# A gelu tail dealt out anew between ScalarE, VectorE and GpSimd, and two sums taken in turns, in the last block of an attention and MLP kernel

## The chip, the cores and the metric

The kernel runs on one core of one Trainium2 chip. The metric is the device time of one execution in microseconds (us). Of several executions the median counts. Beside them stands one profiled execution with its trace.

## The reference

The reference is one transformer layer with adaptive layer norms, for 2048 rows of 512 numbers, all in float32:

```
mod = (silu(c) @ w_mod) -> sa, ca, ga, sb, cb, gb
h = layernorm(x) * (1 + ca) + sa
x = x + ga * attention(h)         # 32 query heads of 16, one key and value head
h = layernorm(x) * (1 + cb) + sb
x = x + gb * (gelu(h @ w1 + b1) @ w2 + b2)     # gelu by tanh; w1 is 512 x 1376
```

What follows is about the last line: the MLP, and in it the gelu and the second product, `@ w2`.

## The kernel before

**Blocks.** The 2048 rows are worked in eight blocks of 256. For each block there is attention, and then a job that the kernel calls `rest`: output projection (`wops`), layer norm, first MLP product (`w1ps`), gelu, second MLP product (`w2ps`), store. While attention of block b runs, TensorE takes small batches of matmuls from the job of block b-1. For the last block, 7, there is no attention left to lie beside; its job runs alone at the end, and many lines in it ask `if fast`. This document is about that end.

**Numbers in two parts.** Each float32 operand of a projection or MLP product is split into a high part, a cast to the narrower `fp32r` type, and a low part, the remainder after that cast. The function `split` (line 128) issues the two instructions: a cast (lines 130 to 134, by engine) and a subtraction (line 137). A product of two such operands is three matmuls: high by high, low by high, high by low. `batches` (line 167) lists these matmuls in order and hands them out in lists of a given size; before a list goes out it asks `ready` whether the last chunk in it has been issued, and gives out a wait of one step (`yield -1`) as long as it has not.

**Chunks.** The 1376 columns of `w1` are 11 chunks of 128 (`NF` = 11, the last one padded). For one chunk, the first product is 12 matmuls with 256 columns (four parts of 512 rows, times three). The first four chunks (`GROUP`) go together, row part by row part, since the parts of the normed input come one after another; chunks 4 to 10 follow one by one. The gelu of one chunk is a 128 x 256 tile and, in the last block, this row of instructions:

| step after the chunk's turn | engine and line | what |
|---|---|---|
| 1 | ScalarE 947 | `z` = sum + bias, out of PSUM |
| 1 | ScalarE 948 | `tt` = its square, scaled, out of PSUM |
| 1 | VectorE 949 | `tt` = (`tt` + 1) * `z` |
| 4 | ScalarE 960 | `tt` = tanh of it, scaled |
| 6 | VectorE 964 | `z` = (`tt` + 1) * `z` |
| 6 | VectorE, by `split`, 134 | `gH` = cast of `z` |
| 6 | VectorE or GpSimd, by `split`, 137 | `gL` = `z` - `gH`: VectorE for even chunks and for 9 and 10, GpSimd for 1, 3, 5 and 7 |

**The second product.** Each of the two 128-row halves of the block is a sum over the 11 chunks, 33 matmuls, in which the gelu is the stationary operand and `w2` the moving one. The first half has 512 columns. The second half is made as two sums of 256 columns, so that the last store is short. The three sums come one after another: all of the first, all of the second, all of the third. Each is then added to the input rows by VectorE (line 1009) and sent out (line 1010).

**What sets the order.** The program is written with a manual schedule: every engine, and the queue of DMAs on SP, runs its instructions in the order in which the Python code issues them, and waits on semaphores for what each needs. That order follows a counter of steps, `clock`. `later(n, fn)` (line 145) appends `fn` to the list `pending` with the step `clock + n`; `due` (line 151) runs everything that has come due, in the order of that list. In the end phase (lines 1471 to 1484) the last job's generator is walked: a list of matmuls is issued at once and takes no step; a number n is n steps, and each step (`tick`) takes one batch of the job that is still open, that of block 6, issues it, counts one on, and runs `due`. Each chunk of the last block's first product ends with `later(1, gelu)` and two steps, so that in step 2f the second product, cast and remainder of chunk f-3 and the tanh of chunk f-2 are issued, and in step 2f+1 the bias, square and first product of chunk f.

**Fillers.** Two gaps at the start of the last block's job, where its operands are still on their way, are filled with what is left of block 6's second product: `TAIL` = (4, 3) gives four steps and then three, one batch each; one more batch of six (`left`, line 914) is put between the transposes (`PARTS`).

**PSUM banks.** The last block's sums take banks in a fixed turn (`spread`, line 728, and `bank`, line 731).

Of the kernel before, what the change touches and what calls it, by code (L numbers as in the profile page):

```python
# [8 lines left out]
F32 = mybir.dt.float32  # L9
F32R = mybir.dt.float32r  # L10
AF = mybir.ActivationFunctionType
ALU = mybir.AluOpType
AX = mybir.AxisListType

P = 128
# [18 lines left out]
BATCH = 6  # L34
SHORT = 4
LONG = (3, 1)
TAIL = (4, 3)
PARTS = (2, 4)
GROUP = 4
NORM_WAIT = 6  # L40
WARM = (4, 16, 2, 5)
# [4 lines left out]
def raw(ap):  # L46
    return ap.bitcast(F32)
# [3 lines left out]
def adaln_mqa_mlp(  # L51
# [15 lines left out]
    nc = tc.nc  # L67
    _, S, D = x.shape
# [10 lines left out]
    NF = (F + P - 1) // P  # L79
# [4 lines left out]
    blocks = [(r, HQ) for r in range(0, S, HQ)]  # L84
# [43 lines left out]
    def split(dst_h, dst_l, src, eng_h, eng_l, between=None):  # L128
        if eng_h is nc.gpsimd:
            eng_h.tensor_scalar(out=dst_h, in0=src, scalar1=1.0, scalar2=0.0, op0=ALU.mult, op1=ALU.add)  # L130
        elif eng_h is nc.scalar:
            eng_h.copy(dst_h, src)
        else:
            eng_h.tensor_copy(out=dst_h, in_=src)  # L134
        if between:
            between()
        eng_l.tensor_tensor(out=dst_l, in0=src, in1=raw(dst_h), op=ALU.subtract)  # L137
# [7 lines left out]
    def later(n, fn):  # L145
        if draining[0]:
            fn()
        else:
            pending.append((clock[0] + n, fn))
# [17 lines left out]
    def batches(ps, pairs, size, ready=lambda n: True, begin=True, end=True):  # L167

        todo = [(a, b_) for wh, wl, xh, xl in pairs for a, b_ in ((wh, xh), (wl, xh), (wh, xl))]
        last = len(todo) - 1  # L170

        ends = list(range(len(todo), 0, -size))[::-1]
        if ends[0] == 1:
            ends.pop(0)
        for begin_, end_ in zip([0] + ends, ends):
            part = range(begin_, end_)
            while not ready(part[-1] // 3):
                yield -1
            yield [(ps, *todo[n], begin and n == 0, end and n == last) for n in part]

    def whole(batch):
        for ps, a, b_, first_, last_ in batch:
            nc.tensor.matmul(ps, a, b_, start=first_, stop=last_)  # L183
# [622 lines left out]
    def rest_steps(b, fast, rp, bank, ons, ready):  # L806
# [4 lines left out]
        for hf in range(w // HQ):  # L811
# [53 lines left out]
                for h in range(2):  # L865
                    later(3 - 2 * t + 2 * h, lambda t=t, h=h: stats(t, h))
            if fast:
                yield TAIL[0]
                for t in range(2):
                    yield from batches(pss[t], out_pairs(t, [KD - 1]), BATCH, begin=False)  # L870
                    add_x(t, pss[t])
                    stats(t, 0)
                    stats(t, 1)
                    rstd(t, t + 1)
                for t in range(2):
                    xhat(t)
                yield TAIL[1]
            if not fast:
                later(4, lambda: rstd(0, 2))
                later(5, lambda: xhat(0))  # L880
# [31 lines left out]
            if fast:  # L912
                tps = [psum.tile([P, 2, HQ], F32, name=f"tp2_{b}_{hf}_{dp}", **bank()) for dp in range(KD // 2)]
                left = take()
                assert len(left) == sum(PARTS)
                for t in range(2):
                    for dp in range(KD // 2):
                        turn2(dp, tps[dp], t)
                    whole(left[:PARTS[t]])
                    left = left[PARTS[t]:]  # L920
                for dp in range(KD // 2):
                    modulate(dp, tps[dp])
                advance()
                for t in range(2):
                    add_bias(t)
                yield MOD_WAIT
            else:
                for dp in range(KD // 2):
                    ps = psum.tile([P, 2, HQ], F32, name=f"tp2_{b}_{hf}_{dp}", **bank())
                    yield [(ps[:, d2, t * P:(t + 1) * P], xh[:, t, (2 * dp + d2) * P:(2 * dp + d2 + 1) * P], ident,  # L930
                            t + d2 == 0, t + d2 == 2) for t in range(2) for d2 in range(2)]
                    modulate(dp, ps)
                whole_h = clock[0] + 4
                state.update(busy=False, turns=2)
# [7 lines left out]
            def gelu(f, ps):  # L942
                odd = fast and f % 2
                z = rp.tile([P, HQ], F32, name=f"z{b}_{hf}_{f}", tag="wf" if odd else "z", bufs=3)
                tt = rp.tile([P, HQ], F32, name=f"tt{b}_{hf}_{f}", tag="h322" if odd else "tt", bufs=2)
                if fast:
                    nc.scalar.activation(z, ps, AF.Identity, bias=b1c[:, f:f + 1])
                    nc.scalar.activation(tt, ps, AF.Square, scale=GELU_R, bias=b1r[:, f:f + 1])
                    nc.vector.scalar_tensor_tensor(out=tt, in0=tt, scalar=1.0, in1=z, op0=ALU.add, op1=ALU.mult)
                else:  # L950
                    nc.vector.tensor_scalar(out=z, in0=ps, scalar1=b1c[:, f:f + 1], scalar2=None, op0=ALU.add)
                    later(1, lambda: inner(z, tt))

                def inner(z, tt):
                    nc.scalar.activation(tt, z, AF.Square, scale=GELU_R)  # L955
                    nc.gpsimd.tensor_scalar(out=tt, in0=tt, scalar1=1.0, scalar2=1.0, op0=ALU.mult, op1=ALU.add)  # L956
                    nc.gpsimd.tensor_tensor(out=tt, in0=tt, in1=z, op=ALU.mult)  # L957

                def tanh():
                    nc.scalar.activation(tt, tt, AF.Tanh, scale=GELU_C)  # L960

                def last():
                    if fast:
                        nc.vector.scalar_tensor_tensor(out=z, in0=tt, scalar=1.0, in1=z, op0=ALU.add, op1=ALU.mult)
                    else:
                        nc.gpsimd.tensor_tensor(out=tt, in0=tt, in1=z, op=ALU.mult)  # L966
                        nc.gpsimd.tensor_tensor(out=z, in0=tt, in1=z, op=ALU.add)  # L967
                    split(gH[:, f, :], gL[:, f, :], z, nc.vector if fast else nc.gpsimd,
                          nc.vector if fast and (f % 2 == 0 or f > NF - 3) else nc.gpsimd)
                    made.add(f)  # L970

                later(3 if fast else 4, tanh)
                later(5 if fast else 6, last)
# [32 lines left out]
            def store(t, ps, cols=slice(0, D)):  # L1006
                row = row0 + hf * HQ + t * P
                ot = rp.tile([P, D], F32, name=f"ot{b}_{hf}_{t}", tag="ot", bufs=2)
                nc.vector.tensor_tensor(out=ot[:, cols], in0=ps[:, :cols.stop - cols.start], in1=x1[:, t, cols], op=ALU.add)
                send = lambda: nc.sync.dma_start(out=of[row:row + P, cols], in_=ot[:, cols])  # L1010
                if fast:
                    send()
                else:
                    later(2, send)

            while weights:
                yield 2
            for t in range(2):
                sl = slice(t * P, (t + 1) * P)
                for cols in (slice(0, D // 2), slice(D // 2, D)) if fast and t else (slice(0, D), ):  # L1020
                    place = dict(tag="m", bufs=3) if b == len(blocks) - 2 and t else bank()
                    ps = psum.tile([P, D], F32, name=f"w2ps{b}_{hf}_{t}_{cols.start}", **place)
                    ops = [(gH[:, f, sl], gL[:, f, sl], w2H[:, f, cols], w2L[:, f, cols]) for f in range(NF)]
                    size_ = SHORT if b == len(blocks) - 2 and not t else BATCH
                    yield from batches(ps[:, :cols.stop - cols.start], ops, size_, lambda f: made.issuperset(range(f + 1)))
                    if fast:
                        later(1, lambda t=t, ps=ps, cols=cols: store(t, ps, cols))
                        yield 2
                    else:
                        store(t, ps)  # L1030
        stage[b] = 2

    stage = {}
# [127 lines left out]
    def advance():  # L1161

        for job in holder or list(queue):
            while not held and job[0] <= clock[0] and go_on(job):
                pass
            if held or holder:
                break
# [4 lines left out]
    def take():  # L1172
        advance()
        return held.pop() if held else None
# [293 lines left out]
    end_step(*behind)  # L1468
    last = queue.pop()[1]

    def tick():

        batch = take()
        if batch:
            whole(batch)
            advance()
        clock[0] += 1
        due()

    for r in last:  # L1480
        if isinstance(r, list):
            whole(r)
        else:
            for _ in range(max(abs(r), 1)):
                tick()
# [33 lines left out]
```

## Time and profile before

| | us |
|---|---|
| median of three runs | 1560.76 |
| the three runs | 1559.91 to 1560.95 |
| the profiled execution, its own time | 1559.96 |
| span of its trace, first to last instruction | 1557.8 |

Busy over that span are TensorE 1541.8 us, VectorE 1401.4, ScalarE 1228.2 and GpSimd 687.2. TensorE's granted clock is 1.00 throughout. The span leaves out 2.2 us of the execution's own time.

In rows of a timeline, the first number is the start in us from the span's start, the second the length in us, then engine, line, operation, and the tiles as output<-inputs with their shapes; in brackets stands how long the engine was idle ahead of it and what ended that. PE is TensorE (PEld its loads of weights), DVE VectorE, ACT ScalarE, POOL GpSimd. A row of a chain has start, length, engine, tile, line and count. A row of waits has who waited for whom, the total in us, the count and the longest. Lengths of instructions that overlap can't be added; the distance between starts tells the pace.

### The profile page before, as it was taken

The numbers are of one execution on the slowest core, as the hardware profiler recorded it, in microseconds if no ns is written. First come the engines' busy times: TensorE is split into PE (matmuls) and PEld (weight loads), VectorE is DVE, ScalarE is ACT, GpSimd is POOL, SyncE is SP. The second block draws the span as 40 slices with busy tenths as digits, with TensorE's granted clock in tenths as the row PEclk, the third lists the DMA queues.
The fourth block names the chain that finished last, engine by engine and source line by source line (L and its number), as shares of the span: only waits on it lengthen the run. The fifth ranks groups of instructions, "written<-read, shape, count | busy, mean of one in ns | idle before, by whom it ended". The sixth has DMA issues, their size and how long they took to land.

```text
span 1557.8 us, 41408 instructions
## 1 busy us (share of the span) xinstructions
PE 1541.8 (99%) x16372; PEld 953.8 (61%) x16372; DVE 1401.4 (90%) x2476; ACT 1228.2 (79%) x2392; POOL 687.2 (44%) x1198
## 2 busy tenths in 40 slices
PE   7999999999999999999999999999999999999999
PEld 4455555567655665557655675556655576556658
DVE  7999999999999999999999999999999999999725
ACT  5577778788878887788877887788877888778963
POOL 5545433867322571246521562245612474225722
PEclk9999999999999999999999999999999999999999
DMA  7235412312030211203112120303112130212241
GB/s 241 101 94 199 146 56 86 124 52 97 19 109 20 83 58 37 94 21 106 31 51 80 55 87 23 108 15 100 44 47 83 35 108 16 74 63 64 83 144 70
DMA packets 83269, 121.61 MB, mean 78 GB/s; under 512 B 19630, under 2 KB 56494, under 8 KB 82820
## 3 DMA queue, kind: packets, MB, share of 16 engines
q1 hardware_dynamic: 83060, 118.97, 23.6%
q8 instruction: 129, 2.11, 0.6%
q14 instruction: 64, 0.52, 0.1%
q10 hardware_dynamic: 16, 0.00, 0.0%
HBM read 91.13 MB, written 27.27 MB: 76 GB/s over the span
## 4 chain that ended last, share of the span: by engine, by line
PE 88%; DVE 10%; DMA 2%; ACT 1%; issue 0%; POOL 0%; SPq 0%; DVEq 0%
PE acc L633 30%; PE m L507 25%; PE e L612 16%; DVE mx L512 8%; PE w1ps L193 8%; PE w2ps L183 2%; PE w2ps L193 2%; PE qps L193 2%; PE w1ps L183 1%; DMA xt<-in_A_x_dram 1%; PE tp L193 1%; PE wops L193 1%; PE kps L162 1%; DVE st L833 1%; DVE x L826 1%; PE idle L287 0%
## 5 line engine op out<-in xcount | busy, mean ns | idle before, releaser
L512 DVE TENSOR_REDUCE mx<-m 128x1 f32<-128x512 f32 x2048 | 1269.1, 681 | 87.0 <-PE m L507 65.7
L616 ACT ACTIVATE p<-e 128x512 f32<-128x512 f32 x2048 | 1098.4, 598 | 253.9 <-PE e L612 115.7
L507 PE MATMUL m<-ks,qst 64*128 64x512 f32 x2048 | 831.4, 429 | 1.6 <-DVE mx L512 0.6
L612 PE MATMUL e<-qst,ks 64*128 64x512 f32 x2048 | 739.9, 412 | 0.0
L633 PE MATMUL acc<-p,va 128*32 128x256 f32 x8192 | 548.0, 385 | 0.0
L507 PEld LDWEIGHTS m<-ks,qst 64*128 64x128 f32 x2048 | 366.2, 184 | 209.8 <-DVE mx L512 174.0
L612 PEld LDWEIGHTS e<-qst,ks 64*128 64x128 f32 x2048 | 358.0, 184 | 92.2 <-ACT p L616 63.6
L633 PEld LDWEIGHTS acc<-p,va 128*32 128x32 f32 x8192 | 213.8, 109 | 214.2 <-issue 110.7
L555 POOL TENSOR_SCALAR mt<-turned 8x32 f32<-8x32 f32 x256 | 53.5, 209 | 417.9 <-DVE turned L561 405.9
L193 PE MATMUL w1ps<-h2H,w1t 64*128 64x256 f32 x1216 | 232.9, 287 | 0.0
L193 PEld LDWEIGHTS w1ps<-h2H,w1t 64*128 64x128 f32 x1216 | 183.5, 185 | 28.5 <-DVE mx L512 16.9
L193 PE MATMUL w1ps<-h2L,w1t 64*128 64x256 f32 x608 | 167.2, 275 | 0.0
L193 PE MATMUL w2ps<-w2H,gH 64*128 64x512 f32 x264 | 115.9, 439 | 0.0
L193 PEld LDWEIGHTS w1ps<-h2L,w1t 64*128 64x128 f32 x608 | 112.3, 185 | 0.0
L193 PE MATMUL w2ps<-w2L,gH 64*128 64x512 f32 x264 | 103.5, 392 | 0.0
L193 PE MATMUL w2ps<-w2H,gL 64*128 64x512 f32 x264 | 102.9, 390 | 0.0
L956 POOL TENSOR_SCALAR tt<-tt 128x256 f32<-128x256 f32 x77 | 31.2, 405 | 141.1 <-ACT tt L955 107.9
L137 POOL TENSOR_TENSOR gL<-z,gH 128x256 fp32r<-128x256 f32 x81 | 60.6, 748 | 17.4 <-DVE gH L134 11.0
L957 POOL TENSOR_TENSOR tt<-tt,z 128x256 f32<-128x256 f32 x77 | 56.9, 739 | 6.4
L967 POOL TENSOR_TENSOR z<-tt,z 128x256 f32<-128x256 f32 x77 | 56.5, 734 | 6.0
L966 POOL TENSOR_TENSOR tt<-tt,z 128x256 f32<-128x256 f32 x77 | 56.7, 736 | 0.0
L193 PE MATMUL wops<-woH,onH 64*128 64x512 f32 x112 | 49.7, 443 | 0.0
(188 smaller groups left out, 1505.0 us busy)
## 6 DMA issues: line engine op xcount, KB each, us to landing
w1t<-dw SPq DMA_DIRECT2D x82, 512.0 KB
qst<-dq SPq DMA_DIRECT2D x384, 32.0 KB
do<-oc SPq DMA_DIRECT2D x64, 128.0 KB
dw<-w1s SPq DMA_DIRECT2D x11, 512.0 KB
xt<-in_A_x_dram SPq DMA_DIRECT2D x4, 1024.0 KB
dq<-qH SPq DMA_DIRECT2D x16, 256.0 KB
dq<-qL SPq DMA_DIRECT2D x16, 256.0 KB
x<-in_A_x_dram SPq DMA_DIRECT2D x8, 512.0 KB
```

The costliest lines, as they stand in the source:

```text
L137: eng_l.tensor_tensor(out=dst_l, in0=src, in1=raw(dst_h), op=ALU.subtract)
L183: nc.tensor.matmul(ps, a, b_, start=first_, stop=last_)
L193: ins = nc.tensor.matmul(ps, a[rows], b_[rows], start=first_ and s == 0, stop=last_ and s == 1)
L507: nc.tensor.matmul(m, qsts[u][rows, j, t * P:(t + 1) * P], ks[rows, kc * 512:(kc + 1) * 512], start=True, stop=True)
L512: nc.vector.tensor_reduce(out=self.mx[u][:, i, kc:kc + 1], in_=m, axis=AX.X, op=ALU.max)
L555: nc.gpsimd.tensor_scalar(out=mt[:, g:g + 32], in0=turned[g:g + 4 * T, :], scalar1=1.0, scalar2=0.0, op0=ALU.mult, op1=ALU.add)
L612: nc.tensor.matmul(e, ks[rows, kt * P:(kt + 1) * P], rhs, start=True, stop=True)
L616: ins = nc.scalar.activation(dst, e, AF.Exp, scale=0.25)
L633: ins = nc.tensor.matmul(accs[u][32 * cidx:32 * cidx + 32, :], va[:, kt, :], rhs, start=kt == 0, stop=kt == NKT - 1)
L957: nc.gpsimd.tensor_tensor(out=tt, in0=tt, in1=z, op=ALU.mult)
L966: nc.gpsimd.tensor_tensor(out=tt, in0=tt, in1=z, op=ALU.mult)
L967: nc.gpsimd.tensor_tensor(out=z, in0=tt, in1=z, op=ALU.add)
```

## The change

Four things change, all in the last block or in the end phase.

- The number of steps in the two gaps is unchanged, four and three, but the matmuls of block 6 are dealt out to them by number: 5, 4, 4, 4 and 6, 6, 6. A new function `some` takes them one by one out of the batches. A plain step no longer takes a batch.
- For chunks 0 to 8 the high part `gH` is made by ScalarE (`nc.scalar.copy`), issued in the place where the cast stood.
- For the same chunks the low part `gL` is made by VectorE, one step later, for odd and even chunks alike. Chunks 9 and 10 keep VectorE for both, as before.
- The three sums are issued in pieces: chunks 0 to 5 of the first sum, chunks 0 to 5 of the second, chunks 6 to 10 of the first, chunks 6 to 10 of the second, then the whole third sum.

```
-TAIL = (4, 3)
+TAIL = ((5, 4, 4, 4), (6, 6, 6))
+SOON = 6
...
-                yield TAIL[0]
+                yield from ((n,) for n in TAIL[0])
...
-                yield TAIL[1]
+                yield from ((n,) for n in TAIL[1])
...
-                    split(gH[:, f, :], gL[:, f, :], z, nc.vector if fast else nc.gpsimd,
-                          nc.vector if fast and (f % 2 == 0 or f > NF - 3) else nc.gpsimd)
+                    if fast and f < NF - 2:
+                        nc.scalar.copy(gH[:, f, :], z)
+                        later(1, low)
+                    else:
+                        split(gH[:, f, :], gL[:, f, :], z, *[nc.vector if fast else nc.gpsimd] * 2)
+                        made.add(f)
+
+                def low():
+                    nc.vector.tensor_tensor(out=gL[:, f, :], in0=z, in1=raw(gH[:, f, :]), op=ALU.subtract)
                     made.add(f)
...
+            parts = [(0, slice(0, D)), (1, slice(0, D // 2)), (1, slice(D // 2, D))] if fast else [(t, slice(0, D)) for t in range(2)]
+            sums = {}
+
+            def second(n, fs):
+                t, cols = parts[n]
                 sl = slice(t * P, (t + 1) * P)
+                if n not in sums:
                     place = dict(tag="m", bufs=3) if b == len(blocks) - 2 and t else bank()
+                    sums[n] = psum.tile([P, D], F32, name=f"w2ps{b}_{hf}_{t}_{cols.start}", **place)
+                ops = [(gH[:, f, sl], gL[:, f, sl], w2H[:, f, cols], w2L[:, f, cols]) for f in fs]
+                size_ = SHORT if b == len(blocks) - 2 and not t else BATCH
+                yield from batches(sums[n][:, :cols.stop - cols.start], ops, size_,
+                                   lambda k: made.issuperset(range(fs[k] + 1)), fs[0] == 0, fs[-1] == NF - 1)
+                if fs[-1] < NF - 1:
+                    return
+                if fast:
+                    later(1, lambda: store(t, sums[n], cols))
+                    yield 2
+                else:
+                    store(t, sums[n])
+
+            for n, fs in ([(0, range(SOON)), (1, range(SOON)), (0, range(SOON, NF)), (1, range(SOON, NF)), (2, range(NF))]
+                          if fast else [(0, range(NF)), (1, range(NF))]):
+                yield from second(n, fs)
...
+    spare = []
+
+    def some(n):
+
+        for _ in range(n):
+            if not spare:
+                spare.extend(take())
+            whole([spare.pop(0)])
+            if not spare:
+                advance()
+
     def tick():
 
-        batch = take()
-        if batch:
-            whole(batch)
-            advance()
         clock[0] += 1
         due()
...
+        elif isinstance(r, tuple):
+            some(*r)
+            tick()
```

More of the change, by code (lines that the diff above doesn't have):

```diff
@@ L914, in rest_steps @@
                 left = take()
-                assert len(left) == sum(PARTS)
+                assert not spare and len(left) == sum(PARTS)
                 for t in range(2):
@@ L1017, in rest_steps @@
                 yield 2
-            for t in range(2):
+            parts = [(0, slice(0, D)), (1, slice(0, D // 2)), (1, slice(D // 2, D))] if fast else [(t, slice(0, D)) for t in range(2)]
+            sums = {}
+            def second(n, fs):
+                t, cols = parts[n]
                 sl = slice(t * P, (t + 1) * P)
-                for cols in (slice(0, D // 2), slice(D // 2, D)) if fast and t else (slice(0, D), ):
+                if n not in sums:
                     place = dict(tag="m", bufs=3) if b == len(blocks) - 2 and t else bank()
[L1022 to L1030, printed above, removed]
+                    sums[n] = psum.tile([P, D], F32, name=f"w2ps{b}_{hf}_{t}_{cols.start}", **place)
[13 more added lines that the diff above has]
+                yield from second(n, fs)
         stage[b] = 2
```

## The prediction

> **What bounds the kernel now.** The page comes first, for the span, then the chain that ended last, for the stage that the change touches. The profiled execution took 1559.96 us, 2.2 us more than its span; the median of the three runs shown is 1560.76 us.
>
> ```profile
> span 1557.8 us, 41408 instructions
> ```
> ```profile
> 1522.91 15.31 PE w1ps L183 x132
> 1538.23 16.52 PE w2ps L183 x99
> 1554.78 0.42 DVE ot L1009
> ```
>
> The last stage is TensorE from 1522.91 us on: 132 matmuls of the last block's first MLP product, then 99 of the second, then one store. Nothing but this stage's length can move. Two more views say how full TensorE is in it: the waits from 1526 to 1547 us, and TensorE's own timeline (start, length, line, what).
>
> ```profile
> PEld w2ps L183 <- DVE gH L134: 1.0, 3, 0.4
> PEld w2ps L183 <- DVE gL L137: 0.8, 3, 0.3
> ```
> ```profile
> 1538.07 0.39 PE L183 MATMUL w2ps<-w2H,gH 128*128 128x512 f32 x1
> ...
> 1543.57 0.45 PE L183 MATMUL w2ps<-w2H,gH 128*128 128x512 f32 x1
> 1543.98 0.50 PE L183 MATMUL w2ps<-w2H,gL 128*128 128x512 f32 x1
> ...
> 1546.22 0.51 PE L183 MATMUL w2ps<-w2H,gL 128*128 128x512 f32 x1
> 1546.80 0.28 PE L183 MATMUL w2ps<-w2H,gH 128*128 128x256 f32 x1
> ...
> 1554.46 0.28 PE L183 MATMUL w2ps<-w2L,gH 128*128 128x256 f32 x1
> ```
>
> Read the starts. Between the first two rows lie 24 matmuls of 512 columns in 5.50 us, 0.229 us each: chunks 0 to 7 of the first sum run without a gap. Chunks 8, 9 and 10 are nine matmuls and take 3.23 us (1543.57 to 1546.80) where nine times 0.229 is 2.06 us. So **1.17 us is all that TensorE waits** for the gelu; the rows of waits (1.0 and 0.8 us) count partly hidden weight loads. The 66 matmuls of 256 columns behind it start 7.66 us apart over 65 steps, 0.118 us each, and end in step at 1554.58 us. The work itself is 33 times 0.229 and 66 times 0.118, 15.34 us, so no order of these matmuls gains more than 1.17 us. The gelu, on the other hand, may get longer without limit, and three chunks of it already come last.
>
> How the gelu runs is in the timelines of ScalarE (ACT) and VectorE (DVE). Per chunk there are: Identity (z, L947), Square (L948), first product (L949), tanh (L960), second product (L964), cast to the high part (L134), remainder for the low part (L137).
>
> ```profile
> 1529.83 0.50 ACT L948 ACTIVATE tt<-w1ps,b1r 128x256 f32<-128x256 f32 x1
> ...
> 1535.28 0.42 ACT L960 ACTIVATE tt<-tt 128x256 f32<-128x256 f32 x1 [0.58 <-DVE tt L949]
> 1535.61 0.46 ACT L947 ACTIVATE z<-w1ps,b1c 128x256 f32<-128x256 f32 x1
> 1535.96 0.47 ACT L948 ACTIVATE tt<-w1ps,b1r 128x256 f32<-128x256 f32 x1
> ...
> 1539.32 0.42 ACT L960 ACTIVATE tt<-tt 128x256 f32<-128x256 f32 x1
> 1539.63 0.47 ACT L947 ACTIVATE z<-w1ps,b1c 128x256 f32<-128x256 f32 x1
> 1540.23 0.48 ACT L948 ACTIVATE tt<-w1ps,b1r 128x256 f32<-128x256 f32 x1
> ```
> ```profile
> 1530.36 0.43 DVE L949 SCALAR_TENSOR_TENSOR tt<-tt,z 128x256 f32<-128x256 f32 x1 [0.61 <-ACT tt L948]
> 1530.70 0.42 DVE L964 SCALAR_TENSOR_TENSOR z<-tt,z 128x256 f32<-128x256 f32 x1
> 1531.16 0.29 DVE L134 CAST gH<-z 128x256 fp32r<-128x256 f32 x1
> 1531.49 0.43 DVE L137 TENSOR_TENSOR gL<-z,gH 128x256 fp32r<-128x256 f32 x1
> ...
> 1533.16 0.97 DVE L964 SCALAR_TENSOR_TENSOR z<-tt,z 128x256 f32<-128x256 f32 x1
> ...
> 1534.83 0.42 DVE L949 SCALAR_TENSOR_TENSOR tt<-tt,z 128x256 f32<-128x256 f32 x1
> ...
> 1545.74 0.42 DVE L137 TENSOR_TENSOR gL<-z,gH 128x256 fp32r<-128x256 f32 x1
> ```
>
> The first ScalarE row is chunk 2's Square, the last one chunk 10's: 10.40 us for eight chunks, 1.30 us each. TensorE makes a chunk of the first product in 12/132 of 15.31 us, 1.39 us, so ScalarE keeps up; VectorE and the rows behind 1540.23 us set the rest. What matters for the change is the order on VectorE: chunk 2's first product at 1530.36 us, and only then chunk 0's second product at 1530.70 us, because each engine runs its instructions in the order in which the steps issued them.
>
> **The change part by part.** *The tuples in the gaps* (5, 4, 4, 4 and 6, 6, 6 in place of four and three batches): the four batches were 4, 4, 3 and 6 matmuls, 17 in all, and the three are 18 in all. The matmuls, their order, and the step in which block 6's store, the last heads' product and the norm are issued stay the same on every queue, SP's too: the store (L1009) follows the 8th matmul, in step 2, both ways. Cost nothing, on either side of nothing: with every queue's order kept there is no place for a gain or a loss.
>
> *The order of the second product* moves work under the waits. The 18 matmuls of 256 columns of chunks 0 to 5 (18 times 0.118, 2.12 us) now stand ahead of the first sum's chunk 6, so chunk 10's low part isn't needed until 1538.07 + 4.13 + 2.12 + 4 times 0.69 + 0.23 = 1547.3 us. With the gelu as it is (the last remainder starts at 1545.74 us) no wait would be left: minus 1.17 us by itself. The accumulators cost nothing: the second sum's bank is the one that chunk 5 leaves, read out some 7 us before.
>
> *The gelu's tail* is where I see the price. Gone: nine VectorE casts and four POOL remainders. New: nine ScalarE copies, and remainders of chunks 0 to 8 on VectorE a step later. Counting busy time this is a relief for VectorE. But the copy sits in ScalarE's queue. Steps issue by the list of what is due: in the even step the copy of chunk f-3 (queued when chunk f-3 began) goes ahead of the tanh of chunk f-2; in the odd step come Identity and Square of chunk f. The copy needs chunk f-3's second product, that stands on VectorE behind chunk f-1's first product, and that needs chunk f-1's Square, the instruction just ahead of the copy on ScalarE. **So ScalarE waits for the end of its own last result, round two engines, once per chunk**, and behind the waiting copy are queued the tanh, the next Identity and the next Square.
>
> The round is priced from starts in the rows above, and from the one ScalarE cast in the trace that has VectorE on both its sides and TensorE behind it:
>
> ```profile
> 1513.70 0.42 DVE L671 TENSOR_TENSOR os_last<-os_last 128x256 f32<-128x256 f32 x1 [0.96 <-DMA os_last<-dr]
> 1514.59 0.42 DVE L137 TENSOR_TENSOR onL<-os_last,onH 128x256 fp32r<-128x256 f32 x1 [0.47 <-ACT onH L132]
> ```
> ```profile
> 1514.16 0.40 ACT L132 CAST onH<-os_last 128x256 fp32r<-128x256 f32 x1 [7.93 <-DVE os_last L671]
> ```
> ```profile
> 1514.61 0.49 PE L183 MATMUL wops<-woH,onH 128*128 128x512 f32 x1 [0.54 <-ACT onH L132]
> ```
>
> - Square to first product: 1529.83 to 1530.36, 0.53 us.
> - First to second product: 1530.36 to 1530.70, 0.34 us.
> - Second product to copy: VectorE to ScalarE, 1513.70 to 1514.16, 0.46 us; 1534.83 to 1535.28 is 0.45. I take 0.45.
> - Copy to tanh: not in the trace. Nearest is the first start behind a wait, 1535.28 to 1535.61, 0.33 us; bounds 0.31 (1539.32 to 1539.63) and 0.40, the cast's whole length.
> - Tanh to Identity 0.31 us; Identity to Square 1535.61 to 1535.96, 0.35 us.
>
> Sum: 2.31 us per chunk instead of 1.30, of which ScalarE idles about 0.95 us ahead of each copy. The Trainium skill (ScalarE: Activation LUTs, "What ACT_TABLE_LOAD costs") gives an ACTIVATE with immediate scale and bias 186 ns plus 0.833 ns per element, neighbours overlapping by 93 ns; for 256 elements that is an estimate of 0.31 us from start to start, and by it the total below would be 0.2 us less. The cast's 0.40 us agrees with its 0.40 us without the overlap.
>
> From chunk 2's Square at 1529.83 us, which nothing delays, eight rounds give chunk 10's Square at 1548.31 us, against 1540.23. Copy f starts 1.32 us after Square f+2; the remainder 0.43 us behind the copy (1514.16 to 1514.59); TensorE takes a low part 0.48 us behind the remainder's start (1545.74 to 1546.22), and then needs 0.58 us until the next chunk may start (1546.22 to 1546.80). Hence on TensorE:
>
> - Chunks 0 to 3 in step. Chunk 5's copy 1542.70, low part taken 1543.61, chunk ends 1544.19.
> - The second sum's chunks 0 to 5: to 1546.31. Chunk 6 (copy 1545.01) is there: 1547.00.
> - Chunk 7: copy 1547.32, taken 1548.23, ends 1548.81. Chunk 8: copy 1549.63, taken 1550.54, ends 1551.12.
> - Chunks 9 and 10 keep VectorE's cast. VectorE from chunk 8's remainder on, at 1550.06: second product 0.34 behind it (tanh 9, from 1549.96, is over by then), cast 0.46 (1530.70 to 1531.16), remainder 0.33 (1531.16 to 1531.49), then second product, cast and remainder of chunk 10 by the same steps: 1552.32. Taken 1552.80, ends 1553.38.
> - 15 and 33 matmuls of 256 columns, 48 times 0.118: 5.66 us, to 1559.04 us.
>
> Against 1554.58 us that is **4.46 us later**; the store and its transfer follow as before. The waits in the second product grow from 1.17 to about 5.6 us although its order is better. Against the profiled 1559.96 us the sum is 1564.4 us; against the median, which lies 0.8 us higher, 1565.2 us. That is my forecast. A tenth of a microsecond on the round moves the end by 0.8 us (eight rounds).
>
> **The rivals.** *The other side, not slower: the copies don't hold up ScalarE, and TensorE alone sets the end.* The mechanism is VectorE's relief. For it speaks this pair:
>
> ```profile
> 1533.05 0.79 POOL L137 TENSOR_TENSOR gL<-z,gH 128x256 fp32r<-128x256 f32 x1 [4.58 <-DVE gH L134]
> ```
>
> While POOL's remainder ran, VectorE's second product at 1533.16 us took 0.97 us, against 0.42 us otherwise. Four such pairs cost VectorE about 2.2 us, and the change removes all four. The Trainium skill (SBUF — State Buffer, "SBUF: two separate sides") says that a VectorE instruction with two SBUF inputs and a GpSimd one that reads SBUF exclude each other for the whole instruction; by that rule, too, all four delays go. The trace agrees: 0.97 against 0.42. If the gelu then goes at TensorE's pace, the 1.17 us go and the time is 1559.6 us. The point from which it decides: the round must be under 1.75 us (2.31 less 4.46/8) not to lose, and near 1.62 us to gain all. Against it: 0.53, 0.34 and 0.45 us, 1.32 us, are crossings that VectorE's freedom doesn't shorten, and ScalarE's own three further starts need 0.99 us. Chance 0.08.
>
> *The tanh fills the gap.* If the due list gave the tanh of chunk f-2 ahead of the copy of chunk f-3, it would run inside the 0.95 us, the round would be 2.00 us, and the end 8 times 0.31 us earlier: plus 2.0 us, 1562.8 us. For it: nothing in the trace of before fixes the two, since the copy isn't there. Against it: the list is kept in the order in which entries were made, and chunk f-3's is the older. Chance 0.09.
>
> *The part does nothing* (order of the second product alone counts) gives the first rival's time and is held in its chance.
>
> **How the numbers follow.** Forecast 0.83, rivals 0.08 and 0.09. A difference under 0.2%, 3.1 us, is about what a measurement of this kernel can tell from no change; the forecast falls under it if the round is below 2.14 us, for which I leave 0.06 of the 0.83: slower 0.77. Within 0.2% are that 0.06 and both rivals, 0.23, less 0.01 for faster by over 3.1 us, for which 1.17 us of waits leave no room that I can see: 0.22 and 0.01. The range: low 1562.3 us takes in the second rival; high 1567.2 us is a round of 2.56 us, with a copy at its whole 0.40 us, 0.53 us instead of 0.45 for the crossing and a tenth for waits on two semaphores.
>
> **What would show it.** Right: Squares some 2.3 us apart from chunk 2 on, chunk 10's near 1548.3 us; ScalarE idle about 0.95 us ahead of each copy, put down to VectorE's z; VectorE's second products all near 0.42 us and POOL without remainders; TensorE's waits for high and low parts at chunks 5, 7, 8, 9 and 10 (at 4 a little), 5 to 6 us in all. Wrong: Squares under 1.75 us apart, or a second product of 99 matmuls that ends within 15.5 us of its start. The gaps would be wrongly costed if TensorE waited more than the 0.54 us that its row at 1514.61 us shows.

## The result, and the profile after

| | median, us | executions |
|---|---|---|
| before | 1560.58 | 13 |
| changed | 1564.46 | 13 |

The ratio is 1.0025, with a 95% interval of 1.0017 to 1.0034: the change makes the kernel 3.9 us slower (2.7 to 5.3 us). The forecast was 1565.2 us, 4.46 us slower.

The profiled execution of the changed kernel took 1568.04 us, more than any other of its 13. About 3.3 us of that lie ahead of the last block's MLP (its first product starts at 1526.04 us, 1522.75 us before), where TensorE's granted clock was 0.50 from 61.8 to 68.5 us in this execution, and 1.00 throughout before; the code that runs there is the same in both, so they don't belong to the change. So everything below is counted from a point inside the last block: from chunk 2's Square, the last one that nothing delays, to the start of the last matmul. Before, that is 1529.83 to 1554.46 us, **24.63 us**; after, 1533.14 to 1562.56 us, **29.42 us**, 4.79 us more.

ScalarE's timeline of the changed kernel (start, length, line, what; in brackets the idle time ahead and what ended it) answers the rows of before in which Squares were 1.30 us apart:

```profile
1533.14 0.49 ACT L949 ACTIVATE tt<-w1ps,b1r 128x256 f32<-128x256 f32 x1
1534.46 0.41 ACT L970 CAST gH<-z 128x256 fp32r<-128x256 f32 x1 [0.83 <-DVE z L965]
1534.77 0.41 ACT L961 ACTIVATE tt<-tt 128x256 f32<-128x256 f32 x1
1535.09 0.46 ACT L948 ACTIVATE z<-w1ps,b1c 128x256 f32<-128x256 f32 x1
1535.45 0.47 ACT L949 ACTIVATE tt<-w1ps,b1r 128x256 f32<-128x256 f32 x1
...
1551.39 0.46 ACT L949 ACTIVATE tt<-w1ps,b1r 128x256 f32<-128x256 f32 x1
```

and VectorE's beside it, with chunk 10's remainder last:

```profile
1533.66 0.43 DVE L950 SCALAR_TENSOR_TENSOR tt<-tt,z 128x256 f32<-128x256 f32 x1 [0.61 <-ACT tt L949]
1534.01 0.42 DVE L965 SCALAR_TENSOR_TENSOR z<-tt,z 128x256 f32<-128x256 f32 x1
1534.90 0.43 DVE L977 TENSOR_TENSOR gL<-z,gH 128x256 fp32r<-128x256 f32 x1 [0.47 <-ACT gH L970]
...
1555.37 0.43 DVE L138 TENSOR_TENSOR gL<-z,gH 128x256 fp32r<-128x256 f32 x1
```

Walk the round from row to row, across the two engines: Square 1533.14, first product 1533.66, second product 1534.01, copy 1534.46, tanh 1534.77, Identity 1535.09, Square 1535.45. From the first Square to the last, chunk 10's at 1551.39 us, eight rounds take 18.25 us, **2.28 us each**. ScalarE idles 0.83 us ahead of each copy, nine times. The totals, from the waits between 1530 and 1562 us (who waited for whom: total, count, longest):

```profile
DVE tt L950 <- ACT tt L949: 8.7, 11, 2.9
ACT gH L970 <- DVE z L965: 7.4, 9, 0.8
...
PEld w2ps L184 <- ACT gH L970: 4.2, 4, 1.5
```

The chain that ended last tells the same. Before, it was one piece of 132 and one of 99 matmuls; now it leaves TensorE after 39 matmuls of the first product and goes round the two engines until chunk 8's copy:

```profile
1526.20 4.80 PE w1ps L184 x39
...
1533.66 0.43 DVE tt L950
...
1534.46 0.41 ACT gH L970
...
1553.14 9.71 PE w2ps L184 x57
```

Last, TensorE in the second product, around its waits ahead of chunks 5, 7 and 8 of the first sum, and behind them:

```profile
1544.83 0.40 PE L184 MATMUL w2ps<-w2L,gH 128*128 128x512 f32 x1
1546.31 0.49 PE L184 MATMUL w2ps<-w2H,gH 128*128 128x512 f32 x1 [1.08 <-ACT gH L970]
...
1550.86 0.51 PE L184 MATMUL w2ps<-w2H,gH 128*128 128x512 f32 x1 [0.53 <-ACT gH L970]
...
1553.14 0.60 PE L184 MATMUL w2ps<-w2H,gH 128*128 128x512 f32 x1 [1.08 <-ACT gH L970]
1553.60 0.80 PE L184 MATMUL w2ps<-w2H,gL 128*128 128x512 f32 x1
1554.19 0.63 PE L184 MATMUL w2ps<-w2L,gH 128*128 128x512 f32 x1
1554.62 0.63 PE L184 MATMUL w2ps<-w2H,gH 128*128 128x512 f32 x1
...
1557.02 0.28 PE L184 MATMUL w2ps<-w2H,gH 128*128 128x256 f32 x1
...
1562.56 0.28 PE L184 MATMUL w2ps<-w2L,gH 128*128 128x256 f32 x1
```

The waits ahead of chunks 5, 7 and 8 are where the prediction had them. What it didn't have are the rows from 1553.60 us on: matmuls of 512 columns that start 0.43 us apart and last 0.63 us, though the last remainder, begun at 1555.37 us, is out before chunk 10's turn comes. The view by windows (the stretch and its length, then the busy time of TensorE, its weight loads, VectorE, ScalarE and GpSimd, then TensorE's granted clock, and what the DMAs moved) shows why:

```profile
1549.90:1553.30 3.40, 1.79 (x6) 0.65 (x4) 1.84 (x6) 2.06 (x6) 0.00 (x0) 1.00 0.00 0
```
```profile
1553.60:1554.50 0.90, 0.90 (x3) 0.74 (x3) 0.83 (x3) 0.11 (x1) 0.00 (x0) 0.50 0.00 0
...
1558.00:1562.00 4.00, 4.00 (x37) 4.00 (x36) 0.42 (x1) 0.00 (x0) 0.00 (x0) 1.00 0.27 100
```

**TensorE's clock falls to half speed**, from 1553.4 to 1556.8 us, behind a stretch of 3.4 us in which it was busy for only 1.79. The price can be read from the rows: by the prediction's steps the first sum would end 0.48 + 0.58 us behind the start of the last remainder, at 1556.43 us; the next sum's first matmul starts at 1557.02, 0.59 us later.

### The profile page after: what moved, and what is told of

Its sections match the earlier page's. It is cut to its first block, busy times and chain, and to the rows that moved or that the text cites. A ratio compares the mean times of both kernels' runs of the same rounds, so it can differ in the third digit from the quotient of the medians.

```text
span 1565.9 us, 41397 instructions
## 1 busy us (share of the span) xinstructions
PE 1548.0 (99%) x16372; PEld 955.8 (61%) x16372; DVE 1399.5 (89%) x2471; ACT 1230.4 (79%) x2401; POOL 681.8 (44%) x1194
## 4 chain that ended last, share of the span: by engine, by line
PE 87%; DVE 10%; ACT 1%; DMA 1%; issue 0%; POOL 0%; SPq 0%; DVEq 0%
PE acc L634 30%; PE m L508 25%; PE e L613 16%; DVE mx L513 8%; PE w1ps L194 8%; PE w2ps L184 2%; PE qps L194 1%; DMA xt<-in_A_x_dram 1%; PE w2ps L194 1%; PE tp L194 1%; PE kps L163 1%; PE wops L194 1%; DVE st L834 1%; DVE x L827 1%; PE w1ps L184 0%; PE wops L184 0%
## 5 line engine op out<-in xcount | busy, mean ns | idle before, releaser
L138 POOL TENSOR_TENSOR gL<-z,gH 128x256 fp32r<-128x256 f32 x77 | 56.9, 739 | 6.4
```

## The experiments

Three theories were to be told apart. The *round theory*: the copy makes ScalarE wait for the result of its own last Square, by way of VectorE, in every step. The *load theory*: nine more instructions are too much for ScalarE, wherever they stand. The *order theory*: taking turns between two sums is what costs. All edits are made to the changed kernel. "Stage" is the time from chunk 2's Square to the last matmul's start in the profiled execution, with its difference from the 24.63 us of before; the ratio is that of the times.

| kernel | Squares apart, us | stage, us | median, us | before beside it, us | ratio, 95% interval |
|---|---|---|---|---|---|
| before | 1.30 | 24.63 | | 1560.58 | |
| changed | 2.28 | 29.42 (+4.79) | 1564.46 | 1560.58 | 1.0025 (1.0017 to 1.0034) |
| order_alone | 1.30 | 23.44 (-1.19) | 1560.04 | 1560.41 | 0.9996 (0.9987 to 1.0005) |
| gelu_alone | 2.28 | 32.48 (+7.85) | 1568.40 | 1560.41 | 1.0048 (1.0036 to 1.0061) |
| copy_later | 1.29 | 23.44 (-1.19) | 1559.53 | 1560.41 | 0.9993 (0.9984 to 1.0002) |
| gaps_undone | 2.28 | 29.30 (+4.67) | 1564.77 | 1560.41 | 1.0028 (1.0017 to 1.0039) |
| tanh_first | 1.98 | 26.37 (+1.74) | 1562.15 | 1560.75 | 1.0008 (0.9999 to 1.0017) |
| waits_filled | 2.28 | 28.83 (+4.20) | 1564.78 | 1560.75 | 1.0028 (1.0017 to 1.0040) |
| copy_twice | 2.72 | 32.75 (+8.12) | 1569.22 | 1560.75 | 1.0057 (1.0044 to 1.0071) |
| no_gpsimd | 1.30 | 24.28 (-0.35) | 1560.48 (one) | 1560.75 | |

### order_alone: the new order with the old casts

```
-                    if fast and f < NF - 2:
-                        nc.scalar.copy(gH[:, f, :], z)
-                        later(1, low)
-                    else:
-                        split(gH[:, f, :], gL[:, f, :], z, *[nc.vector if fast else nc.gpsimd] * 2)
-                        made.add(f)
+                    split(gH[:, f, :], gL[:, f, :], z, nc.vector if fast else nc.gpsimd,
+                          nc.vector if fast and (f % 2 == 0 or f > NF - 3) else nc.gpsimd)
+                    made.add(f)
```

> The new order of the three sums and the new gaps, with the gelu's casts and remainders where they were before (VectorE, GpSimd for odd chunks). Round theory (the copy on ScalarE waits for the result of ScalarE's own last Square, once per chunk): no copy, no round; the 1.17 us that TensorE waited in the second product go, time 0.9 to 1.3 us under before, no wait ahead of a chunk over 0.2 us. Load theory (nine more instructions are too much for ScalarE): the same, 0.9 to 1.3 us under. Order theory (taking turns between two sums is what costs): about 4 us over before.

The stage is 1.19 us shorter. In its chain of waits the second product is one piece again, without a gap:

```profile
1538.78 15.34 PE w2ps L184 x99
```

That is the 15.34 us that the prediction worked out from 33 and 66 matmuls, where before took 16.52. The order does what it was priced at, and the order theory falls. In the times it doesn't show: the median is 0.4 us under before, and the interval reaches from 2.0 us faster to 0.8 us slower.

### gelu_alone: the new casts with the old order

```
-            for n, fs in ([(0, range(SOON)), (1, range(SOON)), (0, range(SOON, NF)), (1, range(SOON, NF)), (2, range(NF))]
+            for n, fs in ([(0, range(NF)), (1, range(NF)), (2, range(NF))]
```

> The new casts and remainders, with the three sums one after the other as before. Round theory: Squares 2.28 us apart as in the changed kernel; all of TensorE's waits for the gelu now stand in the first sum, with nothing of the second to fill them: chunk 10's low part is taken some 14.5 us after the first matmul of the second product, then 0.6 us and 66 times 0.118 us follow, 22.8 us where before took 16.5: 6.3 us over before, up to 8 us if TensorE's clock falls to half for 3.4 us, as it did in the changed kernel's profile. Load theory: 6 us over, too. Order theory: no difference from before.

7.85 us more in the stage, 8.0 us in the median. Squares are 2.28 us apart, as in the changed kernel, so the round has nothing to do with the order of the sums. With nothing to fill the waits, the clock stays at 0.50 from 1546.7 to 1557.0 us, three times as long as was expected:

```profile
1544.00:1546.00 2.00, 1.19 (x3) 0.48 (x3) 1.02 (x3) 1.37 (x4) 0.00 (x0) 1.00 0.00 0
...
1550.00:1553.00 3.00, 2.41 (x6) 1.29 (x5) 2.46 (x7) 1.03 (x3) 0.00 (x0) 0.50 0.00 0
...
1558.00:1562.00 4.00, 4.00 (x36) 4.00 (x35) 0.42 (x1) 0.00 (x0) 0.00 (x0) 1.00 0.09 33
```

The new order thus gives back some 3 us of what the new casts cost (7.85 against 4.79), part of it by the shorter stretch at half clock.

### copy_later: the same copies, two steps later

```
                     if fast and f < NF - 2:
-                        nc.scalar.copy(gH[:, f, :], z)
-                        later(1, low)
+                        later(2, high_low)
...
+                def high_low():
+                    nc.scalar.copy(gH[:, f, :], z)
+                    low()
+
```

> As the changed kernel, but the copy of chunk f-3 and its remainder are issued two steps after its second product: ScalarE then has Identity and Square of chunk f and the tanh of chunk f-1 ahead of the copy. The same nine copies, the same relief of GpSimd. Round theory: the copy finds its operand ready, Squares come at TensorE's pace, 1.4 us apart, nothing waits in the second product: 1.0 to 1.3 us under before. Load theory: ScalarE still has nine more instructions, about 4 us over before. Order theory: about 4 us over.

This is the run that decides between the round and the load. ScalarE has the same nine copies, and GpSimd the same relief; what moves is the copy's place in ScalarE's queue, and with it the remainder's in VectorE's by one step. All of the loss is gone, with 1.19 us gained. Squares are 1.29 us apart in the mean, and 1.33 us from chunk 3 on. There ScalarE has no idle time any more: the copy stands right behind the tanh, and the four instructions of a chunk together take 1.33 us, still less than the 1.39 us that TensorE needs for a chunk of the first product.

```profile
1529.85 0.50 ACT L949 ACTIVATE tt<-w1ps,b1r 128x256 f32<-128x256 f32 x1
...
1538.84 0.60 ACT L949 ACTIVATE tt<-w1ps,b1r 128x256 f32<-128x256 f32 x1
1539.20 0.55 ACT L961 ACTIVATE tt<-tt 128x256 f32<-128x256 f32 x1
1539.50 0.54 ACT L976 CAST gH<-z 128x256 fp32r<-128x256 f32 x1
1539.80 0.61 ACT L948 ACTIVATE z<-w1ps,b1c 128x256 f32<-128x256 f32 x1
1540.17 0.61 ACT L949 ACTIVATE tt<-w1ps,b1r 128x256 f32<-128x256 f32 x1
```

The load theory falls. By the trace it shares the shortest stage, 23.44 us, with order_alone. Its median is the lowest, 0.9 us under before; the interval of the times, 0.9984 to 1.0002, still takes in no difference.

### gaps_undone: the two gaps as before

```
-TAIL = ((5, 4, 4, 4), (6, 6, 6))
+TAIL = (4, 3)
...
-                yield from ((n,) for n in TAIL[0])
+                yield TAIL[0]
...
     def tick():
 
+        batch = take()
+        if batch:
+            whole(batch)
+            advance()
         clock[0] += 1
```

> As the changed kernel, with the two gaps dealt out in batches as before. All theories that I hold: nothing changes, each engine's order is the same; 3 to 5 us over before, Squares 2.28 us apart. Gap theory (part of the loss comes from the gaps): over 0.5 us less than the changed kernel's 3.9 us. It also shows whether TensorE's clock falls to 0.50 again in the second product: if it does, 0.6 us longer than without.

It has the same instructions in the same order on every engine as the changed kernel, so it is a second kernel with the same work: stage 29.30 and 29.42 us, medians 1564.77 and 1564.46 us. The stage begins behind the gaps; what shows their cost are the medians, and TensorE's way from the last `wops` piece of its chain to the first product: 8.15 us here (1515.60 to 1523.75) and 8.11 in the changed kernel (1517.93 to 1526.04). The new gaps cost nothing that can be seen. The clock falls again, for 3.4 us from 1550.8 us on, at chunk 8 as in the changed kernel:

```profile
1551.40:1554.00 2.60, 2.60 (x7) 1.97 (x7) 1.97 (x6) 0.02 (x1) 0.00 (x0) 0.50 0.00 0
```

### tanh_first: the second rival, made

```
                     if fast and f < NF - 2:
-                        nc.scalar.copy(gH[:, f, :], z)
-                        later(1, low)
+                        later(1, high_low)
...
+                def high_low():
+                    nc.scalar.copy(gH[:, f, :], z)
+                    low()
+
```

`later(1, ...)` puts the copy behind the tanh of the same even step and ahead of the next Identity; its remainder keeps its place on VectorE.

> As the changed kernel, but in each even step the tanh of chunk f-2 is issued ahead of the copy of chunk f-3, so that it runs while the copy waits. Round theory: the round loses the tanh's 0.32 us, Squares 1.97 us apart in place of 2.28, chunk 10's Square 8 times 0.31 us, 2.5 us, earlier; waits in the second product shrink from 5 to about 2.5 us: 1.5 to 2.2 us over before. Load theory (number of ScalarE's instructions) : as the changed kernel, 4 us over, since their number is the same.

Squares 1.98 us apart, the stage 1.74 us longer than before, the median 1.4 us: near what the prediction had for this rival (2.00 us and 2.0 us), though the interval of the times still takes in no difference from before. One instruction moved over another on ScalarE is worth 0.30 us a round, 2.4 us in eight; the stage is 3.05 us shorter than the changed kernel's, since the clock, too, stays at 1.00. The round is there still, shorter by the tanh:

```profile
1530.31 0.49 ACT L949 ACTIVATE tt<-w1ps,b1r 128x256 f32<-128x256 f32 x1
...
1546.12 0.46 ACT L949 ACTIVATE tt<-w1ps,b1r 128x256 f32<-128x256 f32 x1
```

### waits_filled: TensorE kept busy

Ahead of chunks 5, 7 and 8 of the first sum stand 4, 2 and 4 matmuls that compute nothing: they write to the bank that the third sum overwrites afterwards.

```
-            for n, fs in ([(0, range(SOON)), (1, range(SOON)), (0, range(SOON, NF)), (1, range(SOON, NF)), (2, range(NF))]
+            def fill(k):
+                yield [(sums[2], gH[:, 0, 0:P], w2H[:, 0, :], True, True)] * k
+
+            if fast:
+                for n in range(3):
+                    sums[n] = psum.tile([P, D], F32, name=f"w2ps{b}_{hf}_{n}_s", **bank())
+                for n, fs in [(0, range(5)), (4, None), (0, range(5, 6)), (1, range(6)), (0, range(6, 7)), (2, None),
+                              (0, range(7, 8)), (4, None), (0, range(8, NF)), (1, range(6, NF))]:
+                    yield from second(n, fs) if fs else fill(n)
+            for n, fs in ([(2, range(NF))]
```

> As the changed kernel, with idle matmuls (512 columns, into the third sum's bank, which the third sum overwrites later) ahead of chunks 5, 7 and 8 of the first sum: 4, 2 and 4 of them, in the waits that the changed kernel's trace shows there (1.25, 0.70 and 1.25 us), about 0.23 us each. They compute nothing. Clock theory (TensorE's waiting in the second product is what brings its clock to 0.50 behind it): the granted clock stays at 1.00, chunks 9 and 10 go in steps of 0.23 to 0.46 us, and the end is 0.4 to 0.6 us earlier than the changed kernel's: 3.3 to 4 us over before. Rival (the clock falls for another reason, or the gelu alone sets the time): the clock falls again, no gain. Squares 2.28 us apart either way.

The granted clock stays at 1.00 through the whole of the second product. Here are two windows at the place where the changed kernel and gaps_undone have their fall:

```profile
1550.00:1552.00 2.00, 1.83 (x6) 0.92 (x6) 1.78 (x5) 0.74 (x3) 0.00 (x0) 1.00 0.00 0
1552.00:1554.00 2.00, 2.00 (x10) 1.28 (x10) 1.05 (x4) 0.00 (x0) 0.00 (x0) 1.00 0.00 0
```

and the stage is 28.83 us: 0.59 us under the changed kernel's and 0.47 under gaps_undone's, with the same round. More matmuls, and sooner done. (In this execution the first product took 15.76 us from first to last start, as in those of gelu_alone and copy_twice, and 15.20 in the others; the reason stays open, and the stage doesn't feel it, since in these three the round is slower than the first product.)

In the times nothing shows: 4.0 us over the before beside it, where the changed kernel was 3.9 over its own. The list of executions gives a reason why there may be little to show. A fall of 3.4 us to 0.50 takes 0.001 from the mean clock of 1562 us. Of the changed kernel's 13 executions ten have a mean clock of 1.000, with a median of 1564.28 us; two have 0.999, with 1565.31 and 1565.35 us; the profiled one, which has the early fall too, 0.997. In gaps_undone three of seven have 0.999, among them the profiled one, whose trace has the fall. So most executions seem to have no such fall. That is read off rounded means; a trace exists of the profiled executions alone.

It also weakens what this run shows: one execution without a fall could be chance. The means of all the kernels support the clock theory better. Below 1.000 are 6 of the 72 executions of order_alone, copy_later, tanh_first and the befores beside the experiments, 6 of 20 of the changed kernel and gaps_undone, and all 9 of gelu_alone and copy_twice, where TensorE waits longest. The more it waits, the oftener the clock falls; that the waiting is the cause is well supported, and not shown beyond doubt.

### copy_twice: one suspected cost doubled

```
                         nc.scalar.copy(gH[:, f, :], z)
+                        nc.scalar.copy(gH[:, f, :], z)
                         later(1, low)
```

> As the changed kernel, with ScalarE's copy issued twice in a row for each of the chunks 0 to 8. Round theory: the second copy adds its start to start, 0.31 us, to each round: Squares 2.59 us apart, chunk 10's Square 2.5 us later, the end 2.5 us later by the gelu and up to 1 us more by a clock that stays low for longer: 6.5 to 8 us over before. If ScalarE had idle time to spare in the round, nothing or less than 1 us over the changed kernel.

Chunk 10's remainder comes 26.16 us behind chunk 2's Square (1530.71 to 1556.87 us), against 22.23 us in the changed kernel: 3.93 us for nine copies, more than a round of 2.59 us would give. The round is 2.72 us. The expectation had the second copy 0.31 us behind the first, as a tanh comes; the trace has 0.44 us, the first one's whole length and a little:

```profile
1540.19 0.41 ACT L970 CAST gH<-z 128x256 fp32r<-128x256 f32 x1 [0.83 <-DVE z L965]
1540.63 0.41 ACT L971 CAST gH<-z 128x256 fp32r<-128x256 f32 x1
1540.94 0.41 ACT L961 ACTIVATE tt<-tt 128x256 f32<-128x256 f32 x1
```

The two write the same tile, and the next instruction, that doesn't, follows in 0.31 us; whether the shared tile is the reason was not tested. The size was off by 0.13 us a copy; the sign and the mechanism hold: whatever stands in the round is paid in every turn. The stage grew by only 3.33 us over the changed kernel's, because the clock's fall costs nothing here: it lasts from 1547.4 to 1550.8 us, while the second sum runs, and TensorE then waits 1.52 us for chunk 8's copy anyway.

### no_gpsimd: what GpSimd's remainders cost

Old order, all casts and remainders on VectorE:

```
-                    if fast and f < NF - 2:
-                        nc.scalar.copy(gH[:, f, :], z)
-                        later(1, low)
-                    else:
-                        split(gH[:, f, :], gL[:, f, :], z, *[nc.vector if fast else nc.gpsimd] * 2)
-                        made.add(f)
+                    split(gH[:, f, :], gL[:, f, :], z, *[nc.vector if fast else nc.gpsimd] * 2)
+                    made.add(f)
...
-            for n, fs in ([(0, range(SOON)), (1, range(SOON)), (0, range(SOON, NF)), (1, range(SOON, NF)), (2, range(NF))]
+            for n, fs in ([(0, range(NF)), (1, range(NF)), (2, range(NF))]
```

> Old order of the three sums, new gaps; casts and remainders of all chunks on VectorE, none on ScalarE or GpSimd. It tells what GpSimd's four remainders cost VectorE. By the rows of before a pair of chunks takes 3.00 us on VectorE with one delay of 0.55 us in it; without GpSimd it has one remainder more: 0.34, 0.46, 0.33 and 0.34 us per chunk, 2.94 us per pair. So all second products near 0.42 us, the gelu no more than 0.3 us earlier, TensorE's wait in the second product 0.9 to 1.2 us as before. If the delay hides more than its 0.55 us, the pair comes under 2.8 us and the wait under 0.7 us.

All 11 second products (line 965 here) take their short time, 0.417 to 0.422 us; the delays of 0.55 us are gone with GpSimd's remainders:

```profile
L965 DVE SCALAR_TENSOR_TENSOR z<-tt,z x11: 417/419/422, 1531.9 to 1545.8; 128x256 f32<-128x256 f32 x11
```
```profile
1532.70 0.43 DVE L138 TENSOR_TENSOR gL<-z,gH 128x256 fp32r<-128x256 f32 x1
1534.16 0.43 DVE L138 TENSOR_TENSOR gL<-z,gH 128x256 fp32r<-128x256 f32 x1
```

The remainders start 1.46 us apart, 2.92 us a pair against 3.00 before. The four remainders that VectorE now makes itself eat nearly all of what the delays had cost, and the stage is 0.35 us shorter, in this one execution. The wait that is left in the second product, about 0.8 us, is a little under the range that was expected.

## Why the prediction was right

- **What bounds it.** Right. TensorE's 1.17 us of waits were all that an order could gain: order_alone and copy_later gain 1.19 us in the trace and not more.
- **The gaps at no cost.** Right, as far as the times tell: gaps_undone. The sign named for the contrary is absent: in the profiled execution of the changed kernel TensorE has no idle time ahead of the `wops` matmul where before had 0.54 us.
- **The round.** Right in its mechanism and, by 0.03 us, in its size: 2.31 us forecast, 2.28 measured. Term by term, from the rows of the first round: Square to first product 0.52 (0.53 forecast), to second product 0.35 (0.34), to copy 0.45 (0.45), to tanh 0.31 (0.33), to Identity 0.32 (0.31), to Square 0.36 (0.35). These add up to 2.31 us; in the later rounds the first step is 0.49 to 0.50 us, and a round takes 2.27 to 2.29. The copy's own step, the one that no row of before had, is 0.31 us, the lower of the two bounds. The Trainium skill (ScalarE: Activation LUTs, "What ACT_TABLE_LOAD costs") has the figures from which the prediction worked out an estimate of 0.31 us for it; the trace agrees. The idle time ahead of each copy is 0.83 us and not 0.95: from Square to copy are 1.32 us, as forecast, and the Square's own 0.49 us go off.
- **The waits in the second product.** Right in their places at chunks 5, 7 and 8. At 9 and 10 the matmuls at half speed fill the time; in waits_filled, at full speed, the low parts of both go 0.46 us behind the high ones, where matmuls in step are 0.23 us apart. Chunk 10's remainder was forecast 22.49 us behind chunk 2's Square (1552.32 less 1529.83) and came 22.23 us behind it (1555.37 less 1533.14), eight rounds of 0.03 us sooner.
- **What was missed: the clock.** The sum held TensorE at full speed. By the same steps with the measured round it would have ended 4.2 us later than before; the profiled stage ended 4.79 us later, and the 0.59 us between the two are the fall to half speed, as the rows at 1555.37 and 1557.02 us show. waits_filled, in which the clock doesn't fall, measures 4.20. In the profiled stage it was partly luck that 4.46 us came so near: two misses of opposite sign (0.26 us too long in the gelu, 0.59 us not counted). In the median, where most executions seem to have no fall, the sum without the gelu's miss, 4.2 us, stands against 3.9.
- **The first rival,** not slower. It failed where the prediction put its condition: the round stayed above 1.75 us. VectorE's relief did come, second products at 0.42 us throughout, but VectorE then waited 8.7 us for Squares (2.9 of them for the first). With the round broken up (copy_later) the rival's result is there.
- **The second rival** fell by the order of the due list, as read: copy, then tanh. tanh_first shows that its price was nearly right.
- **The range** held: 1564.46 us lies between 1562.3 and 1567.2, and 3.9 us is over the 3.1 us that 0.2% are; the interval, from 2.7 us, reaches below that.

## What to carry to other kernels

Moving an instruction to an idler engine isn't priced by busy time: look at what stands ahead of it and behind it in the new engine's queue, and whether what it waits for hangs, by way of other engines, on the instruction just ahead of it. If so there is a round, every step in it is paid once per turn. Here it was cured by issuing the copy two steps later; taking it back, as in order_alone, gave the same stage of 23.44 us, so the copy on ScalarE was worth nothing measurable by itself. Ask also what new waits on TensorE do to its clock in the microseconds behind them.

## What the runs showed of the hardware

In the changed kernel TensorE's granted clock fell to 0.50 although no single wait was longer than about 1.5 us from start to start: in the 3.4 us ahead of the fall it was busy 1.79 us. It stayed down for 3.4 us in the changed kernel, in gaps_undone and in copy_twice, and for about 10.2 us, three times as long, in gelu_alone. In tanh_first the emptiest such stretch had 2.61 us of work in 3.4, and the clock stayed up:

```profile
1544.50:1547.90 3.40, 2.61 (x14) 1.49 (x12) 2.00 (x6) 2.35 (x8) 0.00 (x0) 1.00 0.00 0
```

The Trainium skill (TensorE: Matmul & The Clock Gate, "What's actually happening") describes two speeds, half and full, and a free-running activity window of 3.4 us. The trace agrees on the half and on the 3.4 us. The busy share of just any 3.4 us doesn't decide: in copy_twice TensorE was busy for only 1.18 us between 1542.3 and 1545.7 us, and the clock stayed at 1.00 until 1547.4 us, when it fell behind 1.87 us of work in 3.4. A window that starts at no fixed point of the kernel would fit this, and also that only some executions show a lower mean clock; no run here tests that.
